# Tables for two chunks in one product: a state-space convolution and an MLP on one core of Trainium2

## The chip, the cores and the metric

The kernel runs on one core of one Trainium2 chip. The metric is the device time of one execution in microseconds (us); lower is better. The engines are named as in the profile: PE is TensorE (matrix products; PEld its weight loads), DVE is VectorE, ACT is ScalarE, POOL is GpSimd, SP is the engine that issues most transfers.

## The reference

The input `x` has 2048 positions of 512 channels. The first block is an S4 layer: a diagonal state-space model with 128 states per channel defines a convolution kernel K of 2048 taps for each channel, which is applied to the normalised input by way of a Fourier transform. The second block is an MLP (512 to 1376 to 512).

```python
def _A_ref(u, A_re, A_im, B_re, B_im, C_re, C_im, log_dt, Dskip):
    dt = jnp.exp(log_dt)[:, None]
    A = A_re + 1j * A_im
    ...
    logdA = dt * A
    dB = dt * Bc
    l = jnp.arange(L)                                  # rounded to bfloat16
    P = jnp.exp(logdA[:, :, None] * l[None, None, :])
    K = jnp.einsum("dn,dnl,dn->dl", Cc, P, dB).real
    ...                                                # causal convolution of u with K by FFT, + u * Dskip

def _B_ref(x, w1, b1, w2, b2):
    y = _layernorm(x, axis=-1)
    h = _gelu(jnp.einsum("bsd,df->bsf", y, w1) + b1)
    return jnp.einsum("bsf,fd->bsd", h, w2) + b2

h = x + _A_ref(_layernorm(x), ...)
out = h + _B_ref(_layernorm(h), ...)
```

## The kernel before

All data lies in one large SBUF tile, `ar`, cut by byte offsets, so that the profile names nearly every operand `ar`; results of products lie in four PSUM slots, `ps`. The channels form four chunks of 128 (`c` = 0 to 3), two chunks to a half (`hf` or `q` = 0, 1).

**Order.** The program is first recorded as a list of operations (`add`), each with the engine that may run it. A hand-kept list, `ORDER`, then says in which order they are issued. A plain number takes the first engine that the operation allows, its bitwise complement (a negative number) the second. Every engine works off its own part of the list strictly in order. A model of times in `Sched.run` only decides how many filling products (L1379) are put into gaps on TensorE.

**Tables.** The taps K of a channel are split as l = a + b: table A has 20 entries (`NA`) per channel, table B has 33 (`NB`), each with a real part (`EA`, `EB`) and an imaginary part (`IA`, `IB`), with the 128 states on the partitions. Magnitudes come from exponentials on ScalarE (`aexps`, L949 and L952; `bexps`, L732). `chain` makes the phases: TensorE adds up angles in PSUM (L986), ScalarE takes sine and cosine (L988), and VectorE multiplies magnitude by sine and by cosine (L1007 and L1008 for most tables; L993 and L994 for table A of half 1, whose layout has the channels innermost; L1006 changes a sign). There are four chains: B and A of half 0, then B and A of half 1, 60 operations on VectorE.

**Taps.** A product over the 128 states of table A by table B gives the 20 x 33 taps of a channel. For chunks 0 and 1, `kgen` takes two products (real and imaginary) per channel, in four column groups of TensorE, 20 weights and 33 columns; both operands have a step of one table row (256 bytes) between elements. For chunks 2 and 3, `kgen4` takes four channels at once: their tables A, padded from 20 to 32 rows, are 128 weights, and 132 columns hold the B of the four channels, in runs of four; only the blocks on the diagonal are used. The padding is set to zero by a memset in `EA2` (L1301) and copied to `IA2` by a transfer of 768 KB on SP's queue. `evac` moves the results from PSUM into `Kg` (L513 on ScalarE, L515 on VectorE).

**After that.** `kspec` (L1095) multiplies the taps by `W`, seven small matrices that are made from one table of values and 28 masks (four row groups each; L561, a TENSOR_SCALAR per mask and row group, most on GpSimd), and begins the Fourier transform. The result goes through DRAM (`AK_d`) and through `fstage` (L912). `unorm` (L881) normalises the input, `xspec` (L893) transforms it, `inverse` multiplies both (L1135) and transforms back (L1145); SP's queue turns the result by transposing transfers (`turn`, L1151). `tail` (L1214) adds the skip path and `mlp` (L1268, L1270, L1290, L1292) does the second block. `load_mlp` loads its weights over the space of `EA2` and `IA2`.

The lines that call the parts in question, at the end of the kernel function:

```python
for q in range(2):
    for c in (2 * q, 2 * q + 1):
        (kgen if q == 0 else kgen4)(c, 5.1 + 4 * c)
    for n, bs in enumerate(KB[q]):
        kstage(q, AKb[q][n], AK_d[q][n], KF[q][n], bs, 9.2 + 8 * q + n)
```

Of the kernel before, what the change touches and what calls it, by code (L numbers as in the profile page):

```python
# [10 lines left out]
ALU = mybir.AluOpType  # L11
# [139 lines left out]
class VS(V):  # L151
# [93 lines left out]
class Sched:  # L245
# [42 lines left out]
    def run(self, nslots):  # L288
# [13 lines left out]
        for code in ORDER:  # L302
# [16 lines left out]
            if e == "POOL" and o.hv:  # L319
                for a, b in hold:  # L320
                    if a <= s < b:
                        s, end = b, b + c
# [62 lines left out]
def kernel(ctx, tc, A_u, A_A_re, A_A_im, A_B_re, A_B_im, A_C_re, A_C_im, A_log_dt, A_Dskip,  # L385
# [53 lines left out]
    Dz = take(bf16, NCH, 32)  # L439
# [7 lines left out]
    ASZ, BSZ = NA * CW * 2, NB * CW * 2  # L447
    E0 = pos[0]
    EB0 = E0 + 2 * ASZ
    BA0 = E0 + 2 * ASZ + NCH * BSZ  # L450
    IB0 = BA0 + 2 * ASZ
    IA2 = at(BA0 + 2 * ASZ + NCH * BSZ, bf16, 2, 4, 32, 32)
    EA2 = at(IA2.hi, bf16, 2, 4, 32, 32)
    pos[0] = EA2.hi
    HF = 2 * ASZ + 2 * BSZ
# [18 lines left out]
    Kg = [take(bf16, NB, 2, 32), at(sc0 - 512, bf16, NB, 4, 2, 32)]  # L474
    zlo = take(bf16, NB, 2, 32).lo
    AK0 = take(bf16, 16, 2 * CW).lo
    XB = [at(lo + 16384, bf16, 8, 512) for lo in (E0, BA0)]
    PR = [[at(rest0 + 2048 * n, bf16, 8, CW) for n in range(4)], [take(bf16, 8, CW) for _ in range(2)] + [at(lo + 24576, bf16, 8, CW) for lo in (E0, BA0)]]
    Z = [[at(lo, bf16, P, 16) for lo in q] for q in ((zlo, sc0 + 8192), (EA2.lo + 11264, IA2.lo + 11264))]
# [3 lines left out]
    IA = [at(BA0 + c * ASZ, bf16, NA, CW) for c in range(2)]  # L483
# [48 lines left out]
    class Tmp:  # L532
        def __init__(self, lo, hi):
            self.p, self.hi = lo, hi

        def __call__(self, dt, *shape):
            v = V(ar, self.p, dt, shape)
            self.p = (v.hi + GR - 1) // GR * GR
            assert self.p <= self.hi, (self.p, self.hi)
            return v  # L540

    tE = Tmp(BA0, BA0 + HF)
    tL = Tmp(BA0 + HF, IA2.hi)
    ct = tL

    def POOL(cost, f, r=(), w=(), pr=None, hv=1):
# [379 lines left out]
    def dmaj(v, a):  # L926
        return v.ap().rearrange("p c g a i -> p (c g) a i")[:, :, a:a + 4, :]
# [492 lines left out]
```

## Time and profile before

| | |
|---|---|
| median of three runs | 262.47 us (262.35 to 263.89) |
| profiled execution, whole | 262.47 us |
| its span (first to last instruction) | 260.1 us |
| TensorE busy | 230.3 us, 89% of the span, 3236 products |
| VectorE busy | 183.3 us, 368 instructions |
| ScalarE busy | 176.8 us, 214 instructions |
| GpSimd busy | 61.8 us, 234 instructions |
| granted TensorE clock | 0.999 |

Products are pipelined: the duration of one runs from its start to its result, and many overlap, so the rate is read from the starts, not from the durations. A line number can be that of a helper: L513 and L515 are every evacuation from PSUM, L561 is every TENSOR_SCALAR that may go to GpSimd, L571 every TENSOR_TENSOR and L576 every SCALAR_TENSOR_TENSOR made by one helper.

### The profile page before, as it was taken

What the parts mean: (1) busy time and instruction counts of PE and PEld (TensorE: products, weight loads), DVE (VectorE), ACT (ScalarE), POOL (GpSimd) and SP (SyncE); (2) the same over time, 40 slices, a digit from 0 to 9 for tenths busy, and PEclk for the clock granted to TensorE, in tenths of its full rate; (3) what the DMA queues carried; (4) which work ended last, traced back from release to release, by engine and by line L of the source; (5) the groups of instructions that cost most, each with busy time, mean ns of one, the idle gap of its engine ahead of it and who ended that gap; (6) DMA issues with size and microseconds to landing.
All of it is one profiled execution on the core that took longest, in us unless ns stands there. A gap on an engine that the chain in (4) does not pass through costs nothing.

```text
span 260.1 us, 7656 instructions
## 1 busy us (share of the span) xinstructions
PE 230.3 (89%) x3236; PEld 133.7 (51%) x3249; DVE 183.3 (70%) x368; ACT 176.8 (68%) x214; POOL 61.8 (24%) x234
## 2 busy tenths in 40 slices
PE   7215997888997999989999998899999999999994
PEld 3102673454876586444467765555553434444452
DVE  3999997999999964679899778974615676222021
ACT  2679989999977977578989956966514701762700
POOL 9930871699996000000000000000000000000000
PEclk9999999999999999999999999999999999999999
DMA  6940012000001247729835985560771040214202
GB/s 161 211 108 2 4 38 28 3 4 3 3 5 57 72 164 222 249 93 283 279 112 88 143 161 176 97 170 3 117 131 36 0 93 20 61 28 96 69 15 66
DMA packets 40371, 23.88 MB, mean 92 GB/s; under 512 B 25649, under 2 KB 37778, under 8 KB 40338
## 3 DMA queue, kind: packets, MB, share of 16 engines
q1 hardware_dynamic: 39746, 22.95, 36.8%
q10 hardware_dynamic: 592, 0.46, 0.8%
q8 instruction: 25, 0.41, 0.6%
q14 instruction: 8, 0.07, 0.1%
HBM read 10.03 MB, written 6.29 MB: 63 GB/s over the span
## 4 chain that ended last, share of the span: by engine, by line
PE 57%; DVE 25%; ACT 11%; issue 5%; POOL 0%; DVEq 0%; ACTq 0%; POOLq 0%
PE ps L1268 15%; PE ps L1290 15%; PE ps L1145 8%; PE ps L893 5%; ACT ar L988 4%; ACT ar L513 4%; DVE ar L871 4%; PE ps L912 4%; DVE ar L1007 3%; DVE ar L576 3%; DVE ar L571 2%; PE ps L1095 2%; PE ps L1061 2%; DVE ar L1008 2%; DVE ar L559 2%
## 5 line engine op out<-in xcount | busy, mean ns | idle before, releaser
L513 ACT CAST ar<-ps 128x1024 bf16<-128x1024 f32 (+3 forms) x72 | 65.2, 970 | 19.3 <-PE ps L1145 6.9
L1270 ACT ACTIVATE ar<-ps,ar 128x512 bf16<-128x512 f32 (+1 forms) x44 | 28.2, 686 | 36.7 <-PE ps L1268 36.6
L561 POOL TENSOR_SCALAR ar<-ar 128x128 bf16<-128x128 bf16 (+6 forms) x44 | 39.6, 921 | 7.6 <-ACT ar L583 7.3
L1290 PE MATMUL ps<-ar 128*128 128x512 bf16 (+3 forms) x180 | 39.1, 367 | 0.4
L1268 PE MATMUL ps<-ar 128*128 128x512 bf16 (+1 forms) x176 | 39.3, 379 | 0.0
L515 DVE CAST ar<-ps 128x1024 bf16<-128x1024 f32 (+2 forms) x28 | 30.6, 1113 | 11.9 <-ACT ar L513 4.0
L988 ACT ACTIVATE ar<-ps 128x1024 bf16<-128x1024 int16 x36 | 35.1, 1032 | 5.1 <-DVE ar L1007 1.6
L1135 DVE TENSOR_TENSOR ar<-ar 128x1024 bf16<-128x1024 bf16 x48 | 30.7, 687 | 10.3 <-PE ps L1145 9.9
L1292 DVE TENSOR_TENSOR ar<-ps,ar 128x512 bf16<-128x512 f32 (+1 forms) x17 | 11.1, 660 | 37.7 <-PE ps L1290 35.0
L1290 PEld LDWEIGHTS <-ar 128*128 128x128 bf16 (+1 forms) x187 | 17.9, 98 | 20.0 <-issue 0.8
L1268 PEld LDWEIGHTS <-ar 128*128 128x128 bf16 (+1 forms) x176 | 17.3, 100 | 20.5 <-issue 0.8
L986 PE MATMUL ps<-ar 128*32 128x256 f16 x560 | 21.4, 275 | 5.0 <-ACT ar L988 3.1
L1145 PEld LDWEIGHTS <-ar 64*128 64x128 bf16 x768 | 21.6, 94 | 5.4 <-issue 3.0
L1145 PE MATMUL ps<-ar 64*128 64x128 bf16 x768 | 23.9, 217 | 0.3 <-ACT ar L513 0.3
L986 PEld LDWEIGHTS <-ar 128*32 128x32 f16 x560 | 14.3, 97 | 12.5 <-issue 12.2
L912 PE MATMUL ps<-ar 128*64 128x512 bf16 (+1 forms) x160 | 17.7, 342 | 1.2 <-DMA ar<-AK_d 0.6
L732 ACT ACTIVATE ar<-ar 128x1024 bf16<-128x1024 f32 x16 | 15.6, 1041 | 3.2 <-DVE ar L559 3.2
L893 PE MATMUL ps<-ar 128*32 128x512 bf16 x256 | 16.0, 381 | 0.3 <-ACT ar L513 0.3
L576 DVE SCALAR_TENSOR_TENSOR ar<-ar 128x4 f32<-128x4 f32 (+5 forms) x44 | 14.2, 327 | 2.5 <-ACT ar L583 1.4
L583 ACT ACTIVATE ar<-ar 128x512 f32<-128x512 f32 (+8 forms) x18 | 11.9, 681 | 4.9 <-DMA ar<-in_A_log_dt_dram 1.8
L1008 DVE TENSOR_TENSOR ar<-ar 128x1024 bf16<-128x1024 bf16 x21 | 14.6, 719 | 0.0
L1007 DVE TENSOR_TENSOR ar<-ar 128x1024 bf16<-128x1024 bf16 x21 | 14.5, 716 | 0.1
(99 smaller groups left out, 318.6 us busy)
## 6 DMA issues: line engine op xcount, KB each, us to landing
ar<-AK_d SPq DMA_DIRECT2D x8, 512.0 KB, 5.6
ar<-in_A_u_dram SPq DMA_DIRECT2D x4, 512.0 KB, 9.2
AK_d<-ar SPq DMA_DIRECT2D x2, 1024.0 KB, 4.6
AK_d<-ar SPq DMA_DIRECT2D x4, 512.0 KB, 4.0
out_dram<-ar SPq DMA_DIRECT2D x30, 64.0 KB, 2.0
ar<-in_B_w_dram SPq DMA_DIRECT2D x4, 344.0 KB, 6.0
ar<-in_B_w_dram SPq DMA_DIRECT2D x2, 640.0 KB, 6.6
ar<-ar SPq DMA_DIRECT2D x1, 768.0 KB, 5.4
```

Of the source, the lines that this page charges most:

```text
L513: act.copy(out_fn(), in_fn())
L515: dve.tensor_copy(out_fn(), in_fn())
L561: en.tensor_scalar(a, b, f(s1), f(s2), op0, op1)
L893: pe.matmul(pst(p)[32 * cg:32 * cg + 32, 512 * z:512 * z + 512], lhsT=BD.ap()[:, 32 * f + 2 - 2 * jl:32 * f + 34 - 2 * jl], rhs=un[2 * (2 ...
L912: pe.matmul(pst(p)[64 * h:64 * h + 64, w * (k + r):w * (k + r) + w], lhsT=T.ap()[:, f, r, :], rhs=v[f:f + 1].ap()[:, 0, :], start=True, st ...
L986: pe.matmul(pst(p)[32 * g:32 * g + 32, 256 * j:256 * j + 256], lhsT=W2[DELTAS.index(d)].ap(), rhs=S2[g].ap()[:, ch0:ch0 + 256], start=Fals ...
L988: add("ACT", c_act(1024), lambda e, p=p, sc=sc, cs=cs: act.activation(swo(sc[cs]) if hf and kind == "B" else sc[cs].ap().rearrange("p a b ...
L1135: dve.tensor_tensor(o, a, b_[:, :, ::-1, :] if sw else b_, ALU.mult)
L1145: pe.matmul(pst(p)[:, 512 * h + 128 * k:512 * h + 128 * k + 128], lhsT=q.ap()[rows, 2 * k + r, :], rhs=TP[w].ap()[rows, f0 // 2 + k, :], s ...
L1268: pe.matmul(pst(p)[:fs, 512 * z:512 * z + 512], lhsT=w1s[dc].ap()[:, fc * P:fc * P + fs], rhs=ybuf.ap().rearrange("p (t c) k -> p c t k", ...
L1270: add("ACT", c_act(512, 1), lambda e, p=p, z=z, fc=fc, fs=fs: act.activation(hT.ap()[:fs, fc, :], pst(p)[:fs, 512 * z:512 * z + 512], ACT. ...
L1290: pe.matmul(pst(p)[:, 512 * z + c0:512 * z + c1], lhsT=hT.ap()[:fs, fc, 128 * t:128 * t + 128], rhs=w2s[fc].ap()[:fs, c0:c1], start=(fc == ...
```

## The change

- One `kgen(q)` for both halves: both chunks of a half are taken together. The tables A of two chunks lie 32 rows apart in one piece of memory, so that the weights are 52 rows (20, a gap of 12, 20). Two channels are worked on at a time, one in each of two column groups of 64, and the columns are the 33 entries of B of both chunks, 66 in all, for each channel. Of the four blocks that come out, the two of like chunks are used.
- All tables have one layout, so the special cases for half 1 in `aexps` and `chain` go, and with them the large memset and the padding transfer. Three memsets of 768 elements set the gaps of the tables A to zero.
- `Kg` has the same layout for both halves (`[33, 2, 64]`), evacuated in five pieces for each half. `kspec` reads it with other steps.
- The masks are first spread to 32 columns (one operation), and each `W[v]` is then one TENSOR_TENSOR of 512 elements instead of four TENSOR_SCALARs of 128. All seven, and the three memsets, are issued on GpSimd in the new list.
- One table `TPc` of angles instead of two; the third matrix `TP` is made from it in two halves with the sign changed.
- `unorm` has one buffer of eight pieces for both halves of the input.
- `ORDER` is a new list of 1001 operations (1045 before). Besides what follows from the above, in it six of the eight `unorm` operations that stood among the last table operations on VectorE stand behind them, four parts of `kspec` stand ahead of the first product of half 1 instead of two, and the weights of the MLP are loaded behind the fourth transposing transfer. Storage of several buffers moves.

```diff
 ORDER = [
...
-    EA = [at(E0 + c * ASZ, bf16, NA, CW) for c in range(2)]
+    EAL, IAL = [E0, E0 + A32, EA2, EA2 + A32], [BA0, BA0 + A32, IA2, IA2 + A32]
+    EA = [at(lo, bf16, NA, CW) for lo in EAL]
...
-    Kg = [take(bf16, NB, 2, 32), at(sc0 - 512, bf16, NB, 4, 2, 32)]
+    Kg = [take(bf16, NB, 2, 64), at(sc0, bf16, NB, 2, 64)]
...
+    for lo in (E0, IA2, EA2):
+        gap = at(lo + ASZ, f32, (A32 - ASZ) // 4)
+        add(("DVE", "POOL"), (0.87, 0.8), lambda e, gap=gap: (dve if e == "DVE" else gp).memset(gap.ap(), 0.0), w=[gap], hv=1)
...
+    mskx = ct(bf16, 7, 4, 32)
+    mx = lambda e: (dve.tensor_copy if e == "DVE" else gp.tensor_copy)(mskx.ap().rearrange("p v g c -> p (v g) c"), msk[0:28].ap().unsqueeze(2).to_broadcast([P, 28, 32]))
+    add(("POOL", "DVE"), (0.9, 1.0), mx, r=[msk], w=[mskx], pr=1.55, hv=1)
...
-            if dm:
-                E_, I_ = (lambda b0=b0: dmaj(EA2, b0)), (lambda b0=b0: dmaj(IA2, b0))
...
-    def kgen(c, pr):
...
-    def kgen4(c, pr):
...
+    def kgen(q, pr):
+        kg = Kg[q]
+        Ar, Ai = (at(lo[2 * q], bf16, 32 + NA, CW) for lo in (EAL, IAL))
+        xs = [lambda d, lo=lo + 2 * q * BSZ: multi(lo, BSZ, bf16, 2, NB, CW)[:, :, :, d].rearrange("p c k -> p k c") for lo in (EB0, IB0)]
+        i0 = 0
+        for n, h in enumerate((7, 7, 6, 6, 6)):
+            S.pr = pr + 0.01 * n
+            p = Ps()
             for b in range(2):
+                def fn(e, p=p, i0=i0, h=h, b=b):
                     for jj in range(h):
+                        for m, (A_, x) in enumerate(zip((Ar, Ai), xs)):
+                            for g in range(2):
+                                d = 64 * g + i0 + h * b + jj
+                                o = pst(p)[64 * g:64 * g + 32 + NA, 512 * b + 66 * jj:512 * b + 66 * jj + 66].rearrange("p (k c) -> p k c", c=2)
+                                pe.matmul(o, lhsT=A_.ap()[:, :, d], rhs=x(d), start=(m == 0), stop=(m == 1), tile_position=(0, 64 * g))
...
+            evac(ofn, ifn, 132 * h, [p], [kg])
+            i0 += 2 * h
...
-    pads = lambda v: v.ap().rearrange("p c g a i -> p (c g) a i")[:, :, NA:32, :]
-    add("DVE", 1.0, lambda e: dve.memset(pads(EA2), 0.0), w=[EA2], pr=0)
...
     for v in range(7):
-        for g in range(4):
-            PTS(W[v], valW, msk[4 * v + g:4 * v + g + 1], n=128, oap=lambda v=v, g=g: W[v].ap()[:, :, 32 * g:32 * g + 32], pr=2.05)
+        TT(W[v], valW, mskx[v], ALU.mult, n=512, mode=2, oap=lambda v=v: W[v].ap().rearrange("p t (g c) -> p t g c", g=4), aap=lambda: valW.ap().unsqueeze(2).to_broadcast([P, 4, 4, 32]),
+           bap=lambda v=v: mskx[v].ap().unsqueeze(1).to_broadcast([P, 4, 4, 32]), pr=2.05, eng="POOL")
...
-    dma("SP", lambda: pads(IA2), lambda: pads(EA2), 786432, [EA2], [IA2], pr=3.45)
```

More of the change, by code (lines that the diff above doesn't have):

```diff
@@ L321, in run @@
                     if a <= s < b:
-                        s, end = b, b + c
+                        s, end = b, b + c + 0.3
                 late = [a for a, _ in hold if s < a < end]
@@ L438 @@
     DD = take(bf16, 2, 16, 4)
-    Dz = take(bf16, NCH, 32)
+    Dz = take(bf16, 2, 64)
     b1_bf = take(bf16, 11)
@@ L447 @@
     ASZ, BSZ = NA * CW * 2, NB * CW * 2
+    A32 = 32 * CW * 2
+    APR = A32 + ASZ
     E0 = pos[0]
[L449 to L455, printed above, removed]
+    EB0 = E0 + APR
+    BA0 = EB0 + NCH * BSZ
+    IB0 = BA0 + APR
+    IA2 = IB0 + NCH * BSZ
+    EA2 = IA2 + APR
+    pos[0] = EA2 + APR
+    HF = APR + 2 * BSZ
     hs = [at(pos[0] + 1024 * n, bf16, 512) for n in range(16)]
@@ L532, with __init__ @@
     class Tmp:
-        def __init__(self, lo, hi):
-            self.p, self.hi = lo, hi
+        def __init__(self, lo, hi, hole=(0, 0)):
+            self.p, self.hi, self.hole = lo, hi, hole
         def __call__(self, dt, *shape):
             v = V(ar, self.p, dt, shape)
+            if v.lo < self.hole[1] and v.hi > self.hole[0]:
+                v = V(ar, self.hole[1], dt, shape)
             self.p = (v.hi + GR - 1) // GR * GR
@@ L595 @@
             dma("ACT", lambda: ldt.ap(), lambda: A_log_dt.partition_broadcast(P), 131072, [], [ldt], pr=0)
+    dtb = tE(bf16, 512)
     xv = x_dram.rearrange("(b q j h l) d -> b h q j (l d)", b=2, j=4, h=2, l=2)
@@ L621 @@
     NF = len(FLD)
-    fi, fsh, fmk = ct(i32, NF), ct(i32, NF), ct(i32, NF)
-    fm, fa, fv = ct(f32, NF), ct(f32, NF), ct(f32, NF)
+    fi, fsh, fmk = tE(i32, NF), tE(i32, NF), tE(i32, NF)
+    fm, fa, fv = tE(f32, NF), tE(f32, NF), ct(f32, NF)
     def fld_fn():
@@ L700 @@
     S.pr = 0.2
-    dtb = tE(bf16, 512)
     AC(dtb, ldt, ACT.Exp, tbl=True)
@@ L714, in tr @@
         return p, (lambda: nat(pst(p, bf16)[:, 0:512]))
-    th = tL(f32, 5, 256)
-    thn = lambda: th.ap().rearrange("p h d -> p (h d)").rearrange("p (a q) -> p a q", q=256)[:, 2:5:2, :]
+    th = tL(f32, 4, 256)
     p, pa = tr("are")
-    TT(th[2], p, dtb, ALU.mult, n=256, psum=True, oap=by4(th[2], 0, 256), aap=lambda pa=pa: pa()[:, 0:64], bap=by4(dtb, 0, 256))
-    def th3(e, p=p):
-        for c in range(2):
-            o = th[3].ap().rearrange("p (c e d g) -> p c e d g", c=2, e=8, d=4)[:, c]
-            x = pst(p, bf16)[:, 0:512].rearrange("p (d c g e) -> p c e d g", d=4, c=4, g=4)[:, 2 + c]
-            y = dtb.ap().rearrange("p (c g e d) -> p c e d g", c=4, g=4, e=8)[:, 2 + c]
-            dve.tensor_tensor(o, x, y, ALU.mult)
-    add("DVE", c_dve(256, 1, True), th3, r=[p, dtb], w=[th[3]], hv=0)
-    TT(th[4], p, dtb, ALU.mult, n=256, psum=True, oap=by4(th[4], 0, 256), aap=lambda pa=pa: pa()[:, 64:128], bap=by4(dtb, 256, 512), pr=0.42)
-    TS(th[0:2], th[2:4], -1.0, None, ALU.mult, n=512, pr=0.35)
+    for hf in range(2):
+        TT(th[2 + hf], p, dtb, ALU.mult, n=256, psum=True, oap=by4(th[2 + hf], 0, 256), aap=lambda pa=pa, hf=hf: pa()[:, 64 * hf:64 * hf + 64], bap=by4(dtb, 256 * hf, 256 * hf + 256), pr=0.2 + 0.22 * hf)
+        TS(th[hf], th[2 + hf], -1.0, None, ALU.mult, n=256, pr=0.35)
     def bexps(pr):
@@ L794 @@
     S.pr = 1.5
-    TPc = [at(Kg[0].lo, i32, 8, P), at(Kg[0].lo + 4096, i32, 8, P)]
+    TPc = at(Kg[0].lo, i32, 8, P)
     codD = ct(i32, 2, 16)
@@ L872 @@
     stats(st, nw, 16, 1.0, EPS, 1.25, ln=True)
-    UN = [[X0s[j] for j in range(7)] + [at(zlo + 1024 * b, bf16, 512)] for b in range(2)]
+    UN = [X0s[j] for j in range(8)]
     def unorm(b, pr):
-        un = UN[b]
+        un = UN
         for j in range(8):
@@ L947, in aexps @@
                 add("PE", 1.75 if n < 3 else 0.88, fn, r=[HLt] + [WA[LV.index(LD[4 * n + j])] for j in range(4)] + ([HLg, Ih] if n < 3 else []), w=[p], new=[p] if n < 3 else [])
-                if hf == 0:
-                    add("ACT", c_act(1024), lambda e, p=p, n=n: act.activation(multi(E0 + 4 * n * 256, ASZ, bf16, 2, 4, CW).rearrange("p c a d -> p a c d"), pst(p).rearrange("p (a c d) -> p a c d", a=4, c=2), ACT.Exp),
-                        r=[p, TBL], w=[EA[c][4 * n + z] for c in range(2) for z in range(4)])
-                else:
-                    add("ACT", c_act(1024), lambda e, p=p, n=n: act.activation(dmaj(EA2, 4 * n).rearrange("p x a i -> p a x i"), pst(p).rearrange("p (a x i) -> p a x i", a=4, x=8), ACT.Exp),
-                        r=[p, TBL], w=[EA2])
+                add("ACT", c_act(1024), lambda e, p=p, n=n, hf=hf: act.activation(multi(EAL[2 * hf] + 4 * n * 256, A32, bf16, 2, 4, CW).rearrange("p c a d -> p a c d"), pst(p).rearrange("p (a c d) -> p a c d", a=4, c=2), ACT.Exp),
+                    r=[p, TBL], w=[EA[2 * hf + c][4 * n + z] for c in range(2) for z in range(4)])
     nch = [0]
-    swo = lambda v: v.ap().rearrange("p a (c i g) -> p (a c) i g", c=2, g=4)
-    swi = lambda p: pst(p, i16).rearrange("p (b g i two) -> p b i g two", g=4, i=32, two=2)[:, :, :, :, 0]
     def chain(hf, kind, pr):
-        dm = hf == 1 and kind == "A"
         ch0 = 256 * hf
@@ L987, in chain @@
                 add("PE", 0.55 + (0 if gn else 0.45 if kind == "B" else 1.3), fn, r=[W2, S2, Wm, cst] + ([HLo, I16] if kind == "A" and gn == 0 else []), w=[p], new=[p] if gn == 0 else [])
-                add("ACT", c_act(1024), lambda e, p=p, sc=sc, cs=cs: act.activation(swo(sc[cs]) if hf and kind == "B" else sc[cs].ap().rearrange("p a b -> p (a b)"), swi(p) if hf and kind == "B" else pst(p, i16).rearrange("p (n two) -> p n two", two=2)[:, :, 0], ACT.Sin, scale=SINSC), r=[p, TBL], w=[sc[cs]])
+                add("ACT", c_act(1024), lambda e, p=p, sc=sc, cs=cs: act.activation(sc[cs].ap().rearrange("p a b -> p (a b)"), pst(p, i16).rearrange("p (n two) -> p n two", two=2)[:, :, 0], ACT.Sin, scale=SINSC), r=[p, TBL], w=[sc[cs]])
             mark = [("cg", kind, hf, gn)]
-            if dm:
-                E_, I_ = (lambda b0=b0: dmaj(EA2, b0)), (lambda b0=b0: dmaj(IA2, b0))
-                f_ = [lambda sc=sc, z=z: sc[z].ap().rearrange("p a (x i) -> p x a i", x=8) for z in range(2)]
-                add("DVE", c_dve(1024, 2), lambda e, E_=E_, I_=I_, f_=f_: dve.tensor_tensor(I_(), E_(), f_[0](), ALU.mult), r=[EA2, sc[0]], w=[IA2])
-                add("DVE", c_dve(1024, 2), lambda e, E_=E_, f_=f_: dve.tensor_tensor(E_(), E_(), f_[1](), ALU.mult), r=[EA2, sc[1]], w=[EA2] + mark)
-                continue
             Sx, Cx = (lambda sc=sc: sc[0].ap().rearrange("p e (c d) -> p c e d", c=2)), (lambda sc=sc: sc[1].ap().rearrange("p e (c d) -> p c e d", c=2))
@@ L1046, in kgen4 @@
-    def kgen4(c, pr):
-        Ar, Br, Ai, Bi = EA2[c - 2], EB[c], IA2[c - 2], IB[c]
-        kg = Kg[c // 2]
-        for j0 in range(0, 32, 6):
-            S.pr = pr + 0.01 * (j0 // 6)
-            p = Ps()
-            n = min(6, 32 - j0)
-            h = (n + 1) // 2
+    def kgen(q, pr):
[5 more added lines that the diff above has]
+            S.pr = pr + 0.01 * n
+            p = Ps()
@@ L1166 @@
     hT = at(Kg[0].lo, bf16, NFC, 512)
-    w1s = [at(EA2.lo + 2752 * c, bf16, F) for c in range(4)]
-    w2s = [at(IA2.lo + 1024 * fc, bf16, 512) for fc in range(11)]
+    w1s = [at(IA2 + 2752 * c, bf16, F) for c in range(4)]
+    w2s = [at(IA2 + 11008 + 1024 * fc, bf16, 512) for fc in range(11)]
     ots = [at(sc0 + 8192 + 1024 * n, bf16, 512) for n in range(8)]
@@ L1316 @@
     for v in range(7):
[L1317 to L1319 removed]
+        TT(W[v], valW, mskx[v], ALU.mult, n=512, mode=2, oap=lambda v=v: W[v].ap().rearrange("p t (g c) -> p t g c", g=4), aap=lambda: valW.ap().unsqueeze(2).to_broadcast([P, 4, 4, 32]),
+           bap=lambda v=v: mskx[v].ap().unsqueeze(1).to_broadcast([P, 4, 4, 32]), pr=2.05, eng="POOL")
+    Jk = at(Kg[0].lo + 4096, f32, 8, 64)
     POOL(1.1, lambda: gp.tensor_tensor(Jk.ap(), Jt.ap().unsqueeze(1).to_broadcast([P, 8, 64]), sk.ap().unsqueeze(2).to_broadcast([P, 8, 64]), ALU.mult), r=[Jt, sk], w=[Jk], pr=1.8, hv=1)
[L1321 to L1323 removed]
+    for r in range(2):
+        PTS(TPc, Jk, 1.0, 16384.0 * (1 - r), op1=ALU.add, n=512, oap=lambda r=r: TPc.ap().rearrange("p k (j r) -> p k j r", r=2)[:, :, :, r], pr=1.81)
     chain(0, "B", 2)
@@ L1330 @@
     AC(T, codT, ACT.Sin, n=2048, scale=SINSC, oap=lambda: T.ap().rearrange("p a b c -> p (a b c)"), iap=lambda: low16(codT), tbl=True, pr=2.98)
-    for n, (q, sc) in enumerate(((0, SINSC), (0, -SINSC), (1, SINSC))):
-        AC(TP[n], TPc[q], ACT.Sin, scale=sc, oap=lambda n=n: TP[n].ap().rearrange("p a b -> p (a b)"), iap=lambda q=q: low16(TPc[q]), tbl=True, pr=2.96 + 0.003 * n)
+    tpv = lambda v, r: v.rearrange("p (n r) -> p n r", r=2)[:, :, r]
+    tpo = lambda n: TP[n].ap().rearrange("p a b -> p (a b)")
+    for n, sc in enumerate((SINSC, -SINSC)):
+        AC(TP[n], TPc, ACT.Sin, scale=sc, oap=lambda n=n: tpo(n), iap=lambda: low16(TPc), tbl=True, pr=2.96 + 0.003 * n)
+    for r, sc in enumerate((-SINSC, SINSC)):
+        AC(TP[2], TPc, ACT.Sin, n=512, scale=sc, oap=lambda r=r: tpv(tpo(2), r), iap=lambda r=r: tpv(low16(TPc), 1 - r), tbl=True, pr=2.966)
     AC(valD, codD, ACT.Sin, scale=SINSC, oap=lambda: valD.ap().rearrange("p a b -> p (a b)"), iap=lambda: low16(codD), tbl=True, pr=2.95)
@@ L1344 @@
     for q in range(2):
-        for c in (2 * q, 2 * q + 1):
-            (kgen if q == 0 else kgen4)(c, 5.1 + 4 * c)
+        kgen(q, 5.1 + 8 * q)
         for n, bs in enumerate(KB[q]):
```

81 lines of the change are left out of this document (21 added, 60 removed), and 71 rows, old and new, of the table ORDER.

## The prediction, on record before the changed kernel ran

> **What bounds the kernel now.** I read the page first (its span and its slices), then the chain of waits, then the groups by form, then the timelines of the engines that the change touches. The profiled execution took 262.47 us, which is the median of the three runs shown, so the sums below stand against both; its span is 260.1, and 2.4 us lie around it.
>
> ```profile
> span 260.1 us, 7656 instructions
> PE   7215997888997999989999998899999999999994
> DVE  3999997999999964679899778974615676222021
> ACT  2679989999977977578989956966514701762700
> ```
>
> A slice is 6.5 us. VectorE and ScalarE are full from slice 2 to slice 14 (to about 90 us), TensorE from slice 13 to the end. So there are two stages, and the gate between them shows in the chain of waits of the stretch 60 to 92 us:
>
> ```profile
> 88.63 0.60 DVE ar L994
> 89.23 0.61 DVE ar L993
> 89.94 0.70 DVE ar L994
> 90.68 0.29 PE ps L1061
> ```
>
> Up to 90.6 us the end is set by the 60 table operations of `chain` on VectorE (0.6 to 0.7 us each, 0.4 for the sign changes of L1006), behind them by the sines on ScalarE (L988). The last of them, L994, releases the first product of `kgen4` (L1061). From there TensorE hardly stops until 256.5 us: 165.8 us that follow the gate whatever happens before it. Work taken from TensorE behind the gate counts fully; ahead of it, only past its idle time (22.5 us busy of the 25 us from 66 to 91).
>
> **The products, the core of the change.** Now, chunks 0 and 1 take 512 products of 20 weights by 33 columns in four column groups (`kgen`, L1030 and L1031), and chunks 2 and 3 take 128 products of 128 by 132 (`kgen4`). After it, each pair of chunks takes 256 products of 52 by 66 in two column groups. What one costs is not in the trace; the rows nearest to it are these, by form and from the timeline.
>
> ```profile
> L1030 PE MATMUL ps<-ar 128*20 128x33 bf16 x256 | 10.4, 248 | 0.5 <-ACT ar L988 0.4
> L1145 PE MATMUL ps<-ar 64*128 64x128 bf16 x768 | 23.9, 217 | 0.3 <-ACT ar L513 0.3
> L1061 PE MATMUL ps<-ar 128*128 128x132 bf16 x64 | 9.8, 235 | 0.1
> L1030 PEld LDWEIGHTS <-ar 128*20 128x20 bf16 x256 | 9.0, 124 | 0.4 <-DVE ar L1008 0.4
> L912 PEld LDWEIGHTS <-ar 128*64 128x64 bf16 x160 | 8.0, 108 | 7.6 <-issue 4.7
> ```
> ```profile
> 73.03 0.29 PE L1030 MATMUL ps<-ar 128*20 128x33 bf16 x4
> 73.10 0.29 PE L1031 MATMUL ps<-ar 128*20 128x33 bf16 x4
> 73.17 0.29 PE L1030 MATMUL ps<-ar 128*20 128x33 bf16 x4
> ```
>
> Contiguous operands: 128 columns take 217 ns (L1145), 512 take 380 (L1268), which is 0.42 ns a column over 163 ns. By that 33 columns should take 177 ns; L1030, whose columns lie 256 bytes apart, takes 248. The timeline says the same as a rate: four products, one to each column group, start every 0.069 us, so each group streams 33 single elements in 69 ns, 2.1 ns an element. L1061 reads the same rows in runs of four elements and lies near the contiguous line (219 expected, 235 found). Weights: 32 contiguous columns take 97 ns (L986) and 64 take 108 (L912), so 20 should take 93; strided 256 bytes apart they take 124, which is 1.9 ns a column.
>
> The new product reads 66 columns, each a single element in another row of the table (two chunks, 33 rows), and 52 strided weights. By the rates above a group needs 66 x 2.1 = 138 ns for the columns and 52 x 1.9 = 99 ns for the weights beside them. Two groups run at once instead of four. So a pair of products takes 99 to 138 ns; I take 120, between the two streams, because with two groups in flight the stream may run somewhat faster than with four. 256 products are 128 pairs: 15.3 us for each half (12.7 to 17.7). The other ends: if only the rate of starting counts (69 / 4 = 17.2 ns a product), 4.4 us; if a round of all groups takes 69 ns whatever its columns, 8.8 us.
>
> [...]
>
> Behind the gate, `kgen4` took 128 x 0.0635 = 8.2 us (the starts of L1061 lie 0.127 apart, L1062 between them). Replaced by 15.3: **+6.9** (-3.8 to +9.5). Its evacuations fall from 12 to 5, but VectorE and ScalarE have room there (8.2 and 12.4 us busy of the 16 from 91 to 107), so they count nothing; without that room they would be a gain of up to 5 us (12 of 0.84 on average against 5 of about 0.95).
>
> **Ahead of the gate on TensorE.** `kgen` took 512 x 0.0172 = 8.8 us and becomes 15.3, against 2.5 us of idle time: +4.0. It stands on TensorE's queue between the phase products of the last two chains, so these, their sines and their table operations wait behind it. The new order also draws one more part of `kspec` (48 products of 30 ns, some 1.5 us) ahead of the gate and puts one of 0.9 behind it: -0.6 behind, +0.6 ahead. Together +4.6, none of it if the products are cheap.
>
> **Ahead of the gate on VectorE.** Gone: 24 mask operations on GpSimd, which cost VectorE 0.09 us each (0.77 instead of 0.68 for every other L1007 and L1008), 2.2; four on VectorE at 0.2, 0.8; six L881 that the new order puts behind the gate, at 0.36, 2.2. The evacuations there change by +0.3. Added: seven mask products of 512 elements, all on GpSimd (every one has the first engine in the new list), between 43 us and the end of the first two chains; also the second L561 of 1024 elements, which lay beside BATCH_NORM_STATS2 at 30.87.
>
> ```profile
> 26.16 2.27 DVE L576 SCALAR_TENSOR_TENSOR ar<-ar 128x512 f32<-128x512 f32 x1
> 25.73 2.15 POOL L571 TENSOR_TENSOR ar<-ar 128x928 f32<-128x928 f32 x1 [10.17 <-DVE ar L559]
> 28.57 1.28 POOL L571 TENSOR_TENSOR ar<-ar 128x512 f32<-128x512 f32 x1 [0.70 <-DVE ar L576]
> 64.42 1.01 POOL L1329 TENSOR_TENSOR ar<-ar 128x128 bf16<-128x128 bf16 x1
> ```
>
> The first two lines show the price: an operation with two inputs on GpSimd held VectorE's 0.69 us operation until it was done, 1.6 us lost. The third is a product of the new size, 1.28 us alone; it lost VectorE nothing, beside BATCH_NORM_STATS2. The fourth, of 128 elements, cost the L1008 beside it 0.2 us. So a mask product costs VectorE 0.2 to 1.28; I take 0.95, nearer to its own size: +6.6 (1.4 to 9.0). The moved L561: +0.9 (1.30 instead of 0.41 for the L1006 beside it). Sum on VectorE: -2.2 - 0.8 - 2.2 + 0.3 + 6.6 + 0.9 = **+2.6** (-2.6 to +5.0).
>
> [...]
>
> **The gate.** The two engines overlap: the masks delay the first chains, after which TensorE is late anyway. Between +2.6 (VectorE alone) and +6.6 (TensorE's 4.6 behind 2 us of masks) I take **+5.0**.
>
> **The rest.** The padding transfer (82.04, 768 KB, landing in 5.4 us) is waited for by nothing on the chain; its memset (L1301) ran at 1.13 while VectorE waited for the first transpose: 0. Three memsets of 768 elements on GpSimd instead: 0, up to +1 where one meets an L1006. Half a table of `TPc` less on GpSimd, one more short activation: 0. The setup before 42 us is bound by ScalarE's exponentials, which remain; the reordered list may win or lose 1 us: -0.5, for one copy moved off ScalarE. SP's queue: the weights of the MLP are now issued behind the fourth transposing transfer (it ended at 153.2) instead of from 116.7 on; four of 344 KB and one of 640 KB at 6 to 7 us land by 170 or sooner, and the first L1268 is at 169.9: 0, up to +4 if they are late.
>
> Sum: 6.9 + 5.0 - 0.6 - 0.5 = +10.8, and 262.5 + 10.8 = **273.3 us**.
>
> **Rivals.** *The start of products is what costs, not their columns.* For it: phase products start 4 to a column round without a gap; against it: 248 ns where 177 are expected. The halves take 4.4 us each; behind the gate -3.8, TensorE ahead of it is no longer late, and the gate moves with VectorE: +0.2 if a mask costs 0.6, +2.6 if 0.95. -3.8 + 0.2 - 0.6 - 0.5 = -4.7: 257.8, faster (260.2 with dear masks). It decides from the point where a product takes under 20 ns. *A round is 69 ns whatever it holds.* 8.8 us each: +0.6 behind, VectorE's +2.6 at the gate, -1.1: 264.6. *All is at its dear end*: 138 ns a pair, masks 1.28, weights of the MLP late: 9.5 + 8 - 1.1 + 2 = +18: 281. *The change doesn't do what it says*: the counts follow from the code, so this has no share.
>
> **How the numbers follow.** Strided columns decide (273.3, itself 266 to 279): 0.60. Start rate: 0.22, most of it below 260. A round of 69 ns: 0.12. All dear: 0.06. A difference of 1%, some 2.6 us, is about what a measurement of this kernel can tell from none. Faster by over 1%: 0.19. Within 1% (259.9 to 265.1): the dear masks of the first rival and most of the second, 0.14. Slower: 0.67. The range 257.5 to 281 leaves out the tails on both sides.
>
> **What would show it.** Right: the 52 by 66 products near 300 ns, their pairs 0.1 to 0.14 us apart; 512 of them some 30 us of TensorE; VectorE operations of 1.5 to 2 us beside the masks; the last table operation near 95 us; about 170 us from there to the end. Wrong: pairs 0.04 us apart, or masks that VectorE does not feel; then the span falls below 260.

## The result, and the profile after

The changed kernel takes 289.72 us (median of four runs, 287.97 to 293.4) against 262.45. The ratio, which here and below leaves out executions in a slower state (here the one of 293.4), is 1.102, 95% interval 1.093 to 1.111. Forecast were 273.3 us and a range up to 281. The direction was right, the size was not: of 27 us that were lost, the sum had 10.8.

The profiled execution has a span of 286.2 us (before: 260.1). From its page, the span and the busy tenths in 40 slices of 7.2 us:

```profile
span 286.2 us, 7359 instructions
...
PE   7229985775999999999989998889999999999994
...
DVE  2899999989952491325898898899465985102012
ACT  3989987995624562416898895666642370640710
...
PEclk9999999998775596579999999999999999999999
```

Before, VectorE and ScalarE were full up to the gate. Now VectorE falls to 5, 2 and 4 tenths in slices 12 to 14 (79 to 100 us) and ScalarE to 2 to 6 from slice 10 on, while TensorE is at 9 from slice 11: ahead of the gate, too, TensorE has become the bound. And a row that was all nines before, the granted clock (PEclk), falls to 5 to 8 tenths from slice 10 to slice 18, but for one. The groups by form show the new products (line; operation; operands; count; then busy us and mean ns of one; idle time before them):

```profile
L1012 PE MATMUL ps<-ar 128*52 128x66 bf16 x512 | 38.2, 323 | 1.9 <-DVE ar L992 1.7 <-ACT ar L515 0.2
L1012 PEld LDWEIGHTS <-ar 128*52 128x52 bf16 x512 | 36.1, 192 | 6.4 <-issue 5.8 <-DVE ar L992 0.4
```

What one costs is in TensorE's timeline (start, us, operation, count), here four unbroken stretches of them:

```profile
70.18 4.18 PE L1012 MATMUL ps<-ar 128*52 128x66 bf16 x56 [1.69 <-DVE ar L992]
77.22 5.82 PE L1012 MATMUL ps<-ar 128*52 128x66 bf16 x80
104.95 8.12 PE L1012 MATMUL ps<-ar 128*52 128x66 bf16 x112 [0.23 <-ACT ar L515]
114.83 6.97 PE L1012 MATMUL ps<-ar 128*52 128x66 bf16 x96
```

From first start to last start, the 112 products take 7.8 us. Over all such stretches a product starts every 70.4 ns, a pair of column groups every 141: 18.0 us for a half, where 15.3 were taken. The gate, in the timeline of all engines:

```profile
103.14 1.29 DVE L992 TENSOR_TENSOR ar<-ar 128x1024 bf16<-128x1024 bf16 x2 [0.40 <-ACT ar L978]
...
104.64 0.72 PEld L1012 LDWEIGHTS <-ar 128*52 128x52 bf16 x6 [0.42 <-DVE ar L992]
104.95 0.53 PE L1012 MATMUL ps<-ar 128*52 128x66 bf16 x4 [0.23 <-ACT ar L515]
```

The last table operation ends at 104.4 instead of 90.6, 13.8 us later, and 181.7 us follow instead of 169.5 (to the end of the span), 12.2 more. The stretches ahead of the gate (us; busy time of PE, PEld, DVE, ACT and POOL; granted clock; DMA share; GB/s):

```profile
76.00:80.00 4.00, 4.00 (x56) 3.21 (x56) 2.92 (x5) 1.46 (x2) 3.50 (x5) 1.00 0.00 0
84.00:88.00 4.00, 4.00 (x62) 3.31 (x60) 1.29 (x2) 2.89 (x3) 0.74 (x1) 0.50 0.00 0
88.00:92.00 4.00, 4.00 (x62) 3.32 (x60) 0.44 (x1) 1.04 (x1) 0.00 (x0) 0.50 0.01 4
92.00:96.00 4.00, 4.00 (x62) 3.14 (x62) 0.55 (x1) 1.04 (x1) 0.00 (x0) 0.50 0.00 0
```

TensorE counts as busy in all 16 us, VectorE in 5; at half of its clock TensorE starts about as many products in 4 us (62) as at the full one (56). So the pace of the new products doesn't come from the clock: the 80 products from 77.22 on, most of them at the full clock, start 70.0 ns apart, the 48 from 89.6 on, at half of it, 69.7.

Times read in the same way from this profile and those of the runs below (us from the start of the span):

| kernel | first table operation | first product of kgen | gate | behind it | span |
|---|---|---|---|---|---|
| before | 47.5 | 66.6 | 90.6 | 169.5 | 260.1 |
| changed | 43.4 | 70.2 | 104.4 | 181.7 | 286.2 |
| e3, neighbouring operands | 43.5 | 68.6 | 92.0 | 166.8 | 258.8 |
| e4, masks on VectorE | 42.6 | 68.7 | 103.5 | 181.7 | 285.2 |
| e5, neighbouring in half 1 | 43.5 | 70.3 | 105.5 | 167.0 | 272.5 |
| e6, e3 and e4 together | 42.4 | 67.5 | 87.5 | 168.5 | 256.0 |
| e9, channel outermost | 44.9 | 72.4 | 91.9 | 166.8 | 258.7 |

### The profile page after: what moved, and what is told of

Read it like the earlier page. It is cut to its first block, busy times and chain, and to the rows that moved or that the text cites. A ratio compares the mean times of both kernels' runs of the same rounds, so it can differ in the third digit from the quotient of the medians.

```text
span 286.2 us, 7359 instructions
## 1 busy us (share of the span) xinstructions
PE 252.6 (88%) x3107; PEld 151.3 (53%) x3107; DVE 188.2 (66%) x363; ACT 170.5 (60%) x203; POOL 49.7 (17%) x222
## 5 line engine op out<-in xcount | busy, mean ns | idle before, releaser
L515 ACT CAST ar<-ps 128x1024 bf16<-128x1024 f32 (+3 forms) x65 | 60.7, 988 | 35.3 <-PE ps L1012 17.5
L517 DVE CAST ar<-ps 128x1024 bf16<-128x1024 f32 (+1 forms) x29 | 33.8, 1180 | 33.5 <-PE ps L1012 18.3
L1219 PE MATMUL ps<-ar 128*128 128x512 bf16 (+1 forms) x176 | 40.0, 379 | 0.0
L1012 PE MATMUL ps<-ar 128*52 128x66 bf16 x512 | 38.2, 323 | 1.9 <-DVE ar L992 1.7
L1012 PEld LDWEIGHTS <-ar 128*52 128x52 bf16 x512 | 36.1, 192 | 6.4 <-issue 5.8
L1086 DVE TENSOR_TENSOR ar<-ar 128x1024 bf16<-128x1024 bf16 x48 | 30.2, 686 | 5.1 <-PE ps L1096 4.2
L976 PE MATMUL ps<-ar 128*32 128x256 f16 x560 | 23.9, 306 | 7.2 <-ACT ar L978 7.0
L1219 PEld LDWEIGHTS <-ar 128*128 128x128 bf16 (+1 forms) x176 | 17.3, 100 | 20.2 <-issue 0.4
L976 PEld LDWEIGHTS <-ar 128*32 128x32 f16 x560 | 14.7, 104 | 16.1 <-issue 14.9
L991 DVE TENSOR_TENSOR ar<-ar 128x1024 bf16<-128x1024 bf16 x26 | 20.0, 790 | 4.2 <-ACT ar L978 3.1
L992 DVE TENSOR_TENSOR ar<-ar 128x1024 bf16<-128x1024 bf16 x26 | 19.3, 771 | 1.3 <-POOL ar L595 0.8
L895 PE MATMUL ps<-ar 128*32 128x512 bf16 x256 | 17.8, 417 | 0.3 <-ACT ar L515 0.3
L940 PE MATMUL ps<-ar 128*128 128x512 f16 x24 | 7.8, 446 | 11.0 <-DVE ar L563 10.9
L575 POOL TENSOR_TENSOR ar<-ar 128x512 bf16<-128x512 bf16 (+2 forms) x9 | 15.5, 1739 | 10.7 <-DVE ar L580 8.7
```

What stands on the lines that cost most here:

```text
L515: act.copy(out_fn(), in_fn())
L517: dve.tensor_copy(out_fn(), in_fn())
L895: pe.matmul(pst(p)[32 * cg:32 * cg + 32, 512 * z:512 * z + 512], lhsT=BD.ap()[:, 32 * f + 2 - 2 * jl:32 * f + 34 - 2 * jl], rhs=un[2 * (2 ...
L976: pe.matmul(pst(p)[32 * g:32 * g + 32, 256 * j:256 * j + 256], lhsT=W2[DELTAS.index(d)].ap(), rhs=S2[g].ap()[:, ch0:ch0 + 256], start=Fals ...
L1012: pe.matmul(o, lhsT=A_.ap()[:, :, d], rhs=x(d), start=(m == 0), stop=(m == 1), tile_position=(0, 64 * g))
L1086: dve.tensor_tensor(o, a, b_[:, :, ::-1, :] if sw else b_, ALU.mult)
```

## The experiments

The theory after the result: the new products wait for operands whose elements lie 256 bytes apart, and that alone makes the difference. Its rivals: it is the columns alone, as the prediction's working had it, or the weights alone; the low clock; the masks on GpSimd.

**Columns (e1).** The columns come from neighbouring elements:

```diff
-        xs = [lambda d, lo=lo + 2 * q * BSZ: multi(lo, BSZ, bf16, 2, NB, CW)[:, :, :, d].rearrange("p c k -> p k c") for lo in (EB0, IB0)]
+        xs = [lambda d, lo=lo + 2 * q * BSZ: at(lo, bf16, 66 * 128).ap()[:, 66 * d:66 * d + 66].rearrange("p (k c) -> p k c", c=2) for lo in (EB0, IB0)]
```

> Every product of kgen reads 66 neighbouring elements of its table instead of 66 single elements 256 bytes apart (so the values of the convolution kernel are others; counts and shapes stay). Theory A, the strided columns set the pace: in the changed kernel the products start every 70 ns (140 ns a pair of column groups), at the full clock and at half of it alike, and 66 x 2.1 = 139. Without the stride the pace falls to that of the weights, at most 99 to 105 ns a pair: kgen 25 us or less instead of 37.5, and the time falls to 276 or below. Theory B, the weight loads set it (192 ns each, 52 elements 256 bytes apart): the pace stays near 70 ns a product and the time near 289. Theory C, the low clock alone makes the products slow: the pace follows the clock row and nothing else, time 285 or more.

Measured: 272.34 us, ratio to the kernel before 1.030 (1.023 to 1.037). The stretch of 112 products behind the gate, in TensorE's timeline:

```profile
95.66 5.27 PE L1012 MATMUL ps<-ar 128*52 128x66 bf16 x112 [0.23 <-ACT ar L515]
```

45.1 ns a product instead of 70.4, 90 a pair.

**Weights (e2).** The weights come from neighbouring elements, the columns stay:

```diff
-lhsT=A_.ap()[:, :, d], 
+lhsT=A_.ap().rearrange("p a d -> p (a d)")[:, 52 * d:52 * d + 52], 
```

> Every product of kgen loads 52 neighbouring elements as weights instead of 52 elements 256 bytes apart (other values, same counts); its columns stay strided. Theory A (columns): the pace stays at 70 ns a product, LDWEIGHTS falls from 192 to about 105 ns, time 287 to 290. Theory B (weights): the pace falls to 50 ns or less, the time to 279 or below.

Measured: 275.48 us, ratio 1.046 (1.042 to 1.051):

```profile
97.13 6.53 PE L1012 MATMUL ps<-ar 128*52 128x66 bf16 x112 [0.23 <-ACT ar L515]
```

55.6 ns a product, 111 a pair. Theory A, which was the prediction's, expected no change, so it falls; theory B, the weights alone, falls with the run before. Each operand's stride has its price.

**Both (e3):**

> Columns and weights of kgen both from neighbouring elements (other values, same counts). If strides are all that is dear in the new products, they start every 17 to 30 ns, kgen takes 9 to 15 us instead of 37.5, the granted clock stays at 1.0 in the kgen stretches, and the time falls to 258 to 268, near that of the kernel before (262.5). If something else in the new form is dear (two column groups instead of four, 52 rows of output), the pace stays above 40 ns and the time above 270.

Measured: 260.73 us, ratio 0.990 (0.987 to 0.994):

```profile
92.55 1.95 PE L1012 MATMUL ps<-ar 128*52 128x66 bf16 x112 [0.23 <-ACT ar L515]
```

15.5 ns a product, a pace near that of the prediction's first rival (17.2), and the granted clock is back at 1.00 (60 to 120 us). The 512 products are 512 x 54.9 = 28.1 us shorter; the span falls by 27.4. Two column groups and 52 rows of output cost nothing by themselves: the strides are the whole loss.

**How the two add up (e12, e10).** The same kernel as changed, with 20 strided weights instead of 52:

```diff
-lhsT=A_.ap()[:, :, d], 
+lhsT=A_.ap()[:, 0:NA, d], 
```

> The changed kernel with 20 strided weights in each product of kgen instead of 52 (the rows of one chunk; those of the other are left out), the 66 columns strided as before. If weights and columns share what the strides cost in proportion, the pair takes 111 + (140 - 111) x 20/52 = 122 ns, 61 ns a product. If the weight loads run beside the columns on a path of their own and only 52 of them were too many, the pair takes the 111 ns of the columns alone, 55 to 56 ns a product. If the pace stays at 70, the number of weights doesn't matter, only that they are strided.

Measured in one execution: 278.61 us, and

```profile
100.19 7.00 PE L1012 MATMUL ps<-ar 128*20 128x66 bf16 x112 [0.23 <-ACT ar L515]
```

60.4 ns a product, 121 a pair: between the 111 of neighbouring weights and the 141 of 52 strided ones, nearly in proportion to their number. So the loads of strided weights don't hide wholly beside strided columns: 20 of them add 10 ns, 52 add 30, some 0.5 to 0.6 ns each, though 52 with neighbouring columns take 90. The same in the kernel before:

```diff
-pe.matmul(o, lhsT=Ar.ap()[:, :, d], rhs=Br.ap()[:, :, d], ...
+pe.matmul(o, lhsT=Ar.ap().rearrange("p a d -> p (a d)")[:, NA * d:NA * d + NA], rhs=Br.ap()[:, :, d], ...
```

> The kernel before, whose kgen products (four column groups) load 20 neighbouring elements as weights instead of 20 elements 256 bytes apart (other values in chunks 0 and 1); the 33 columns stay strided. The prediction read its round of 66 to 69 ns as the price of the 33 columns alone, 2.1 ns each: then the pace stays at 16.5 to 17 ns a product. If strided weights and columns share one path, as the pairs of 140, 111 and 90 ns in the earlier runs say, the round falls to 33 x 1.68 = 55 ns, 14 ns a product or less.

Measured in one execution: 260.18 us; in its quick stretches a product starts every 14.1 to 14.3 ns (16.3 to 16.7 before), a round of four groups every 57 instead of 66. Its groups by form (248 and 124 ns before):

```profile
L1030 PE MATMUL ps<-ar 128*20 128x33 bf16 x256 | 9.2, 234 | 0.7 <-ACT ar L988 0.7
...
L1030 PEld LDWEIGHTS <-ar 128*20 128x20 bf16 x256 | 7.7, 105 | 0.0
```

So 33 strided columns alone are worth 57 ns, 1.7 each, as the 66 of e2 are (111 / 66). In the kernel before the four products of a round of 66 to 69 ns start within 19 ns (median of 106 rounds in its trace), so it isn't the starting that takes the time. The 2.1 of the prediction had the weights in it: the 20 strided ones add 9 ns to the round, 0.45 each.

**One half alone (e5).** As in e3, in half 1 only:

```diff
+... if q else multi(lo, BSZ, bf16, 2, NB, CW)[:, :, :, d] ...
+lhsT=A_.ap().rearrange("p a d -> p (a d)")[:, 52 * d:52 * d + 52] if q else A_.ap()[:, :, d], 
```

> Only the second half of kgen (chunks 2 and 3, the one behind the gate) reads neighbouring elements, columns and weights (other values there, same counts); the half ahead of the gate stays strided. If each half costs what its products cost (70.4 against 15.5 ns, 256 of them, 14.1 us), the gate stays at 104.4, the stretch behind it falls from 181.7 to about 167, and the time to 274 to 276. If instead most of the loss comes from the half ahead of the gate (or from the low clock that it leaves behind), the time stays above 280.

Measured: 274.05 us, ratio 1.042 (1.033 to 1.051). The gate stays (105.5), the stretch behind it falls by 14.7 to 167.0, as 14.1 us of products say. The clock is low ahead of the gate, where the strided half is (0.68 from 66 to 84 us, 0.64 from 84 to 106), and full behind it (1.00 from 106 to 140).

**The masks (e4, e6).** Seven numbers of the list of order take their complement, which is VectorE:

```diff
 ORDER = [
...
-229 ... 235
+-230 ... -236
```

> Only the seven mask products move from GpSimd to VectorE; everything else is the changed kernel. Theory M, they stretch the table operations of VectorE beside them by about 0.95 us each and this reaches the gate: VectorE pays 7 x 0.35 = 2.5 instead of 6.6, the last table operation comes 3 to 5 us earlier than at 104.4 and the time falls to 284 to 286. Rival, TensorE is the bound ahead of the gate anyway (256 products of 70 ns): the first product of kgen starts earlier, but the gate moves by less than 1 us, time 288 to 290.

Measured: 286.64 us, ratio 1.086 (1.081 to 1.092). The table operations beside the masks (L575) were stretched as forecast, from 0.68 us to 1.6 and more. From the timeline of the changed kernel:

```profile
67.91 4.76 POOL L575 TENSOR_TENSOR ar<-ar 128x512 bf16<-128x512 bf16 x3
68.41 1.63 DVE L992 TENSOR_TENSOR ar<-ar 128x1024 bf16<-128x1024 bf16 x1
...
69.96 1.66 DVE L991 TENSOR_TENSOR ar<-ar 128x1024 bf16<-128x1024 bf16 x1
```

But taking that away moves the gate by 0.9 us and the span by as much, as the rival says. The time, 286.6, lies between the two forecasts, and the ratios to the kernel before (1.102 and 1.086) say somewhat more than these two profiles; that difference stays unexplained. With TensorE quick the same step shows in full:

> Neighbouring elements in both halves of kgen (other values) and the seven mask products on VectorE. With the cheap products TensorE has room ahead of the gate, so what the masks cost VectorE should now show in full: theory M, 6.6 - 2.5 = 3 to 4 us off the gate (92.0 in the run with neighbouring elements alone), time 256.5 to 258. Rival: the phase products and sines hold the chain there, the gate moves by less than 1 us, time 260 to 261.

Measured: 256.03 us, ratio 0.977 (0.970 to 0.983). From the first table operation to the gate 45.1 us instead of 48.5: the masks are worth 3.4 there. The gate itself is 4.5 earlier; some of the other 1.1 lies ahead of the first table operation, where in e3 the first mask (L575, at 40.6) stretches two operations of L580 from 1.41 to 2.25 us. The span is only 2.8 shorter, since the stretch behind the gate is 1.7 longer; more on that under the clock.

**The clock (e7).** Dense products were put among those of kgen:

```diff
                                 pe.matmul(o, lhsT=A_.ap()[:, :, d], rhs=x(d), ...)
+                        if b == 0:
+                            pe.matmul(pst(p)[:, 512:1024], lhsT=identb.ap(), rhs=hs[15].ap(), start=True, stop=True)
```

> The changed kernel with 64 products more, each 128 weights by 512 neighbouring columns, spread among the products of kgen (one behind every four of the first piece of each pair; their results are overwritten). At the full clock they take 64 x 0.215 = 13.8 us. Theory clock: the clock row stays at 0.9 to 1.0 in the kgen stretches, the pace of kgen's own products stays at 70 ns (it doesn't follow the clock), and the products around them go back to their full speed (L895 59 instead of 66 ns, L976 40 instead of 49), some 5 us back: time 298 to 300. Rival, the low clock costs the kernel nothing: time 302 to 305.

Measured: 329.18 us, ratio 1.250 (1.240 to 1.260), far from both. TensorE's timeline (L1014 is the dense product), and a window:

```profile
110.10 0.61 PE L1014 MATMUL ps<-ar 128*128 128x512 bf16 x1
110.64 0.49 PE L1012 MATMUL ps<-ar 128*52 128x66 bf16 x4
111.06 0.61 PE L1014 MATMUL ps<-ar 128*128 128x512 bf16 x1
```
```profile
110.00:115.00 5.00, 5.00 (x37) 2.10 (x37) 0.00 (x0) 0.00 (x0) 0.00 (x0) 0.50 0.00 0
```

The dense products didn't keep the clock up: it is at half in most of kgen (0.50 from 105 to 120 us). There each takes 0.54 us to the next start, and 0.32 in the stretches at the full clock (84 to 89 and 127 to 131 us). The 54 of them in the trace take 26.6 us, so that 64 take some 32 of the 40 lost. So this run doesn't price the low clock; it shows only that it was low there too.

**A kernel that lays the operands side by side (e8, e9, e11).** In e3 the products read other data than they should; in this kernel they read their own. The tables have the channel outermost (`tbl` builds an access pattern from an offset and pairs of step and count), and everything that fills them writes that order:

```diff
+        xs = [lambda d, q=q: tbl(ebl(q, 66 * d), (2, 33), (1, 2)), lambda d, q=q: tbl(ibl(q, 33 * d), (2, 33), (1, 2))]
...
+lhsT=tbl(A_.lo + 104 * d, (1, 32 + NA)), 
...
+        if q == A32:
+            return tbl(lo0 + 2 * k, (52, 128), (32, 2), (1, 4))
...
+        return tbl(lo0 + 12, (z, 128), (-2, 4), (1, 2)) if rev else tbl(lo0, (z, 128), (2, 4), (1, 2))
...
+act.activation(tbl(EAL[2 * hf] + 8 * n, (1, 4), (32, 2), (52, 128)), pst(p).rearrange("p (a c d) -> p a c d", a=4, c=2), ACT.Exp)
```

> A whole kernel in which both operands of kgen do lie side by side: the tables are laid out with the channel outermost (66 neighbouring columns of the two chunks, 52 neighbouring weights for each channel), the sines and the exponentials are written in that order, the masks are on VectorE, and five operations move a few places in the order. If ScalarE and VectorE write and read runs of 2, 4 and 8 elements at their old speed (0.69 us for a table operation, about 0.9 for a sine or an exponential of 1024), it comes out near the run with neighbouring elements and masks on VectorE: 256 to 260, below the kernel before. If VectorE loses its double rate on such runs (1.1 us for a table operation), the 60 operations on the chain cost 20 us or more ahead of the gate: time 275 or above.

Measured: 296.12 us, ratio 1.128 (1.121 to 1.135). The products have their 15.6 ns and VectorE keeps its rate: 0.73 to 0.74 us for a table operation. (The double rate of the expectation is, in the kernel before, 0.69 us for 1024 bf16 elements, L1135, beside 0.69 for 512 f32 ones, L571; its 1.1 us was an estimate.) But neither theory had thought of the last line of the diff (groups by form):

```profile
L1022 ACT ACTIVATE ar<-ps 128x1024 bf16<-128x1024 f32 x10 | 45.7, 4864 | 0.0
```

Ten exponentials of 4.86 us instead of 1.03, all ahead of the first table operation, which starts at 79.5. One line was changed:

```diff
-tbl(EAL[2 * hf] + 8 * n, (1, 4), (32, 2), (52, 128)), pst(p).rearrange("p (a c d) -> p a c d", a=4, c=2)
+tbl(EAL[2 * hf] + 8 * n, (52, 128), (32, 2), (1, 4)), pst(p).rearrange("p (a c d) -> p d c a", a=4, c=2)
```

> The kernel with the channel outermost again, with one line changed: the ten exponentials that fill the A tables step through four neighbouring elements first, not through channels 104 bytes apart. If the single two-byte elements that ScalarE wrote in the run before are what made them 4.86 us each instead of 1.03 (10 x 3.8 = 38 us, all of it ahead of the gate), they fall to about 1.05 and the time to 256 to 260. If they stay above 2 us, what ScalarE reads (steps of 1024 bytes in PSUM) is what costs, and the time stays above 270.

Measured: 260.82 us, ratio to the kernel before 0.992 (0.988 to 0.996), 0.8% below the kernel before. Its groups by form:

```profile
L1067 DVE TENSOR_TENSOR ar<-ar 128x1024 bf16<-128x1024 bf16 x26 | 18.6, 745 | 0.6 <-ACT ar L1053 0.3
L1066 DVE TENSOR_TENSOR ar<-ar 128x1024 bf16<-128x1024 bf16 x26 | 18.3, 730 | 0.3 <-issue 0.2
...
L1022 ACT ACTIVATE ar<-ps 128x1024 bf16<-128x1024 f32 x10 | 9.5, 1011 | 0.0
```

It was the writing of single elements (4.86 us), not the reading in steps (1.01). A further run moved six operations of the first stage from GpSimd to VectorE in the list of order:

> The channel-outermost kernel of the run before, with six more operations of the first stage on VectorE instead of GpSimd: the four small products that fill DD (32 elements) and the two that form the codes of T (1024 elements). On GpSimd they last 9 us together between 51 and 61 us, and the table operations beside them come out at up to 1.96 us instead of 0.4 to 0.69. On VectorE they should cost 4 x 0.2 + 2 x 0.7 = 2.2 us. If the stretching reaches the gate, the time falls by 1 to 3 us, to 258 to 260; rival, the gate there is set by ScalarE's sines, and the time stays within 1 us of 260.8.

Measured: 261.26 us, ratio 0.996 (0.992 to 0.999); the gate stays at 91.9. The time is as the rival said, but not for its reason. From the first table operation to the gate VectorE is busy in 46.4 of 47.0 us (46.2 in e9), and ScalarE's sines wait for it, 7 us in all. The table operations (L1066, L1067) got 1.6 us shorter together, and VectorE spends the time on the six that it took over.

## Why the prediction was right and wrong

**The pair of products: right mechanism, undersized.** Strided columns were named as the cost, with 120 ns a pair from bounds of 99 and 138; measured 141, 2.7 us more for each half. The failed step is "66 x 2.1 = 138 ns for the columns and 52 x 1.9 = 99 ns for the weights beside them", and the value between the two. The weights don't lie wholly beside the columns: 111 ns with the columns strided alone, 90 with the weights, 141 together. The reason given for 120, that two groups may stream faster than four, doesn't hold either: a strided column takes 1.7 ns in both (57 / 33 and 111 / 66). With e10 the rows of the kernel before come near: 66 columns at 1.7 and 52 weights at 0.45 make 114 + 23 = 137. A single price for every strided element does not: at the 1.25 of the old round (66 ns for 33 + 20 elements) e12 with its 86 would take 107, and it took 121.

**Ahead of the gate on TensorE: the step that failed most.** "Against 2.5 us of idle time: +4.0" credited the idle time of an engine that stands in a chain. With the masks out of the way, strides in both halves move the gate from 87.5 to 103.5 (e6 against e4), 16.0 us for 256 x (70.4 - 15.9) = 14.0 us of products: nothing was hidden, and 2 us came on top. The phase products that stand between them (L976) are 23.9 us busy instead of 21.0, at the lower clock. Against the 8.8 us of the kernel before, the term is about +9 for the products and +2 on top, not +4.0.

**VectorE and the masks: right.** The operations beside them lost 0.8 to 1.0 us to a mask (1.63 to 1.69 instead of 0.68 at 68 to 73 us), and VectorE idled 1.08 for the last one; that makes 6.6 in all, the sum forecast. On VectorE one takes 0.41 (e6), so that moving them should bring 6.6 - 7 x 0.41 = 3.7; the gate came 4.5 earlier. That they disappear behind a late TensorE was said too, and they do: 0.9 us at the gate in the changed kernel.

**The gate as a whole.** +5.0 taken, +13.8 measured, in a path whose every step is a pair of profiles: from before to e6 -3.1 (the first table operation 5.0 earlier, the stretch behind it 1.9 longer), strides +16.0, masks +0.9. The setup, taken at -0.5, gained 4.1 in the changed kernel; the cause stays open.

**Behind the gate.** +6.9 - 0.6 taken, +12.2 measured: strides +14.9 (e3 against changed; 14.1 by the pace), all else -2.7. From start to start kgen takes 18.6 us there instead of 9.7, by which the term is +8.9. (The forecast has a slip here too: by its own numbers 15.3 - 8.2 is +7.1, not +6.9.) What the sum lacked besides is the work beside it: the spectrum's products (L893 before, L895 now) go from 59.4 to 66.5 ns from start to start, 1.8 us. The other 1.5 of the 12.2 are not assigned to anything.

**The clock had no term and no rival.** Groups by form, first the changed kernel, then e3:

```profile
L895 PE MATMUL ps<-ar 128*32 128x512 bf16 x256 | 17.8, 417 | 0.3 <-ACT ar L515 0.3
```
```profile
L895 PE MATMUL ps<-ar 128*32 128x512 bf16 x256 | 15.8, 381 | 0.3 <-ACT ar L515 0.3
```

Two us of busy time here, 2.9 at L976 (23.9 against 21.0) and 1.0 at the 512-column products of L1046 (9.0 against 8.0) are what the low clock took: in the changed kernel 16 products of L976 last 1.04 us at a granted clock of 0.50 (from 88.63) and 0.62 at 1.00 (from 58.32), 16 of L1046 1.89 at 0.50 (from 113.01) and 1.03 at 1.00 (from 103.68). One more pair of profiles prices it behind the gate. In the profiled execution of e6 the clock is low just once in the stretches of kgen and of what follows, from 97.5 to 101.0 us (granted 0.52); L895, which stands there, is busy 17.5 us in all instead of the 15.8 of e3, and the stretch behind the gate is 1.7 longer (168.5 against 166.8). The other three executions of e6 took 255.7 to 256.1 us, this one 257.8. So there the loss seems to reach the end in full. How much did so in the changed kernel, ahead of the gate above all, stays open: the pace alone explains the span from e3 to the changed kernel to within 1 us, but the quick kernel also waits more ahead of the gate, and the run that was to hold the clock didn't. What brings the clock down is not shown here: PE counts as busy in 4.00 of 4.00 us both where the clock was 0.50 (84 to 96 us) and where it was 1.00 (76 to 80).

**The rest.** MLP weights at 0: right (the first product of L1219 waits for no transfer). Of the rivals, the start rate (under 20 ns) and the round of 69 ns are out; "all dear" had the pair nearly right (138) and still came to 281, since it kept the same gate. Of the signs named, pairs of 0.1 to 0.14 us (0.141, at the edge), products near 300 ns (323) and operations of 1.5 to 2 us beside the masks came true; the table operation near 95 and the 170 us behind it did not.

## What to carry to other kernels

Before two small products are merged into one, price the single strided elements of both its operands: here a strided column took 1.7 ns and each strided weight beside it another 0.45 to 0.6, and the same products from neighbouring elements ran 4.5 times as fast. A price for one operand is read from a row only after the other operand is varied. And idle time of an engine that takes turns with others in a chain is no credit for more work on it: here 14.0 us of products moved the gate by 16.0.

## What the runs showed of the hardware that was not expected

- Two column groups, 66 columns and 52 weights a product: 31 ns a pair with both operands from neighbouring elements, 90 with strided weights, 111 with strided columns, 121 with strided columns and 20 strided weights, 141 with both strided. The last is the same at a granted clock of 1.00 and of 0.50 (70.0 and 69.7 ns a product).
- With the new products strided in both operands the granted clock fell to 0.50 (84 to 96 us), though the profile counts TensorE as busy in 4.00 of 4.00 us; in the run with only half 0 strided (e5) it was 0.64 to 0.68 from 66 to 106 us and 1.00 from 106 to 140. With the products before, strided too but small and in four column groups, it was 1.00 (66 to 92 us).
- ScalarE took 4.86 us to write 1024 single two-byte elements 104 bytes apart (e8), 1.01 us to write them in runs of four (e9), while it read PSUM in steps of 1024 bytes. With runs of two (the exponentials of table B) it took 1.12 instead of 1.04.
- VectorE kept its rate on runs of four and eight, and on reversed runs of two: 0.73 to 0.75 us for 1024 elements, against 0.68 to 0.72 on whole rows.
